# Attention pairs: values behind the next pair's transposes, with copies, shifts and plan steps in other slots

## The chip, the cores and the metric

The kernel runs on one core of a Trainium2 chip. The metric is the device time of one execution in microseconds. The core's engines work side by side, each through its own list of instructions in order: TensorE (PE, matmuls and transposes into PSUM), VectorE (DVE), ScalarE (ACT), GpSimd (POOL) and SyncE (SP, which here issues DMAs). They wait for each other through semaphores.

## What is computed

Causal attention over 8 batches, 12 heads, 448 positions and 64 columns per head, then a mixture of 8 experts with one expert per token and room for 80 tokens each:

```python
scores = scale * np.matmul(q, k.transpose(0, 1, 3, 2))
scores = np.where(mask, -1000000000.0, scores)
attn = np.exp(scores - np.max(scores, axis=-1, keepdims=True))
attn = attn / (np.sum(attn, axis=-1, keepdims=True) + 1e-09)
x = np.matmul(attn, v)            # then (B * S, H * D)
expert_idx = np.argmax(x @ w_gate, axis=1)
# per expert the 80 tokens of largest gate weight:
h = np.maximum(x[tok_idx] @ w1[e], 0.0)
out[tok_idx] = gate_w[tok_idx, None] * (h @ w2[e])
```

## The kernel before, in words

Attention takes the heads two at a time: 8 batches of 6 pairs, 48 pairs in a row, and each pair goes through a software pipeline of three periods. Pair i in its own period: its scores are already in PSUM, and for each of seven blocks of queries DVE runs a *shift* (L445: adds the mask, scales, and takes the extreme of each row) and ACT a *power* (L449: the exponential with the row sum). Blocks 0 and 1 are 192 wide, 2 and 3 are 320, 4 and 5 are 448, the last is 64. In the next period PE *transposes* the powers in four groups of four 128x128 blocks (L483), and each group is *copied* from PSUM to the table PT, the first three whole groups by ACT, the fourth partly by ACT and then partly by DVE (L488). In the period after that PE forms the pair's *values* from PT and v (L506, 16 instructions), and DVE copies them to `xu` (L511, the value copy). Meanwhile PE forms the scores of pair i + 1 (L426) as the last thing in period i, and a small remainder of pair i's scores (L433, `first`) as the first.

A period is written out as eight slots, k = 0 to 7 (the loop at L993 to L1051). All engines' instructions are recorded in the order of this text, and each engine runs its own in that order. Tables say what stands in which slot: TSLOT for the four groups of transposes of pair i - 1, COPIED for their copies, SHIFTED for the seven shifts of pair i; power x always stands in slot x. VSLOT and XSLOT of the new version say it for the values and the value copy; before, values stand in slot 0 and the value copy in slot XSLOT.

Beside the pairs a *plan* runs (`batch_plan`, L943): when a batch's six pairs are through, its steps are put into slots counted from the batch's end, eight per period, so that the steps of one batch share the periods of the next: division by the row sums (NORMS: guard and two small copies on ACT, an inversion on DVE), the transposes of the result into rows and their scaled *stores* (ROWS0 and ROWS1: for each of eight pieces the slot of the turn on PE, L602, and of the store on DVE, L621, whose row then goes out through SP), and the selection of tokens (STEPS; EARLY for the last batch but one): gate products `gp`, their copy `gs`, logits `lp`, `lg`, `logit`, the choice of expert, the ranking with a table of the best 80 so far (`r0t` to `c0l`: two turns on PE, the comparison of the table `rl`/`lt` with lower counts, four comparisons `c3w`/`c3l` to `c0w`/`c0l` of weights on PE and DVE, `gt`), and the merging of new entries (`places` to `row`). Steps that write PSUM and the transposes and the values all take their tiles from one pool `ps_g` of four banks, in turn (L86, L92).

POOL splits q and k into high and low halves for the thirds of a batch to come (L370, L402); DVE does so in the first batch. Behind attention comes a tail for the last batch in a written order (TAIL), then the expert stage, whose weights are loaded through SP into buffers that attention frees.

Of the kernel before, what the change touches and what calls it, by code (L numbers as in the profile page):

```python
# [19 lines left out]
QB = 64  # L20
MASKED = -8.0e9
HUGE = 3.0e38
TSLOT = [1, 2, 4, 5]
COPIED = {2: (0, 0), 3: (1, 0), 4: (2, 0), 5: (3, 0), 6: (3, 1)}
SHIFTED = [0, 0, 1, 1, 2, 3, 3]
XSLOT = 2
NORMS = [0, 2, 2]
ROWS0 = [(2, 4), (4, 5), (6, 7), (10, 12)]
ROWS1 = [(26, 28), (28, 29), (34, 36), (42, 44)]
STEPS = {'gp': 12, 'gs': 13, 'lp': 16, 'lg': 20, 'logit': 20, 'shifted': 21, 'chosen': 22, 'sums': 23, 'one_hot': 23, 'weight': 23, 'columns': 23, 'weighted': 24, 'parts': 24, 'r0t': 29, 'r0c': 30, 'r1t': 30, 'r1c': 31, 'rl': 33, 'lt': 36, 'c3w': 36, 'c3l': 37, 'c2w': 38, 'c2l': 39, 'cp': 41, 'ro': 44, 'c1w': 42, 'c1l': 44, 'c0w': 44, 'c0l': 45, 'gt': 49, 'own': 52, 'earlier': 46, 'rank': 53, 'rr': 55, 'places': 60, 'tn': 66, 'tab': 68, 'rp': 70, 'row': 71}  # L30
EARLY = {'gp': 12, 'gs': 13, 'lp': 16, 'lg': 20, 'logit': 20, 'shifted': 21, 'chosen': 22, 'sums': 23, 'one_hot': 23, 'weight': 23, 'columns': 23, 'weighted': 24, 'parts': 24, 'r0t': 29, 'r0c': 30, 'r1t': 30, 'r1c': 31, 'rl': 33, 'lt': 36, 'c3w': 34, 'c3l': 36, 'c2w': 36, 'c2l': 37, 'c1w': 38, 'c1l': 38, 'cp': 39, 'ro': 40, 'c0w': 39, 'c0l': 40, 'gt': 42, 'own': 44, 'earlier': 41, 'rank': 44, 'places': 45, 'rr': 46, 'tn': 49, 'tab': 49, 'rp': 52, 'row': 53}
THIRD = [0, 0, 2, 2, 4, 6, 8]
THIRD_EARLY = [0, 2, 4, 6, 6, 8, 9]
SECOND = [5, 6, 7, 8, 9, 10, 11]
# [13 lines left out]
def attention_then_moe(  # L48
# [194 lines left out]
    lg = keep.tile([P, NT, H * E], F32, name="lg")  # L243
# [722 lines left out]
    with tc.manual_schedule():  # L966
# [25 lines left out]
        parts = []  # L992
        for i, pr in enumerate(pairs):  # L993
            bt = pr.bt
            if pr.p == 0:
                bt.xu = spool.tile([P, NP, S], F32, name="xu", tag="xu")
                bt.sums = spool.tile([P, NO * H + NP], F32, name="sums", tag="sums", bufs=3)
                bt.rl = None
                for other in pairs[i:i + NP]:
                    other.xu, other.sums = bt.xu, bt.sums  # L1000
                if bt.b < B - 1:
                    batch_plan(bt)
            h = i // PH
            if i % PH == 0:
                if i == 0:
                    later_on(4, [lambda: load_third(2)])
                elif h + 2 < NTH:
                    load_third(h + 2)
                if h:
                    load_values(h)  # L1010
                    if h + 1 < NTH:
                        third_plan(h + 1, i * SLOTS + 1)
            if i == 0:
                scores = scores_groups(pr, i)
                scores[0]()
            _, first, afters = scores
            turns = transpose_groups(pairs[i - 1], i - 1) if i else []
            values = values_group(pairs[i - 2]) if i >= 2 else None
            for k in range(SLOTS):
                if k == 0:  # L1020
                    if values:
                        values[0]()
                    first()
                if turns and k in TSLOT:
                    turns[TSLOT.index(k)][0]()
                for x, at in enumerate(SHIFTED):
                    if at == k:
                        if values and k == XSLOT:
                            values[1]()
                        afters[x][0]()  # L1030
                if k < len(afters):
                    afters[k][1]()
                if turns and k in COPIED:
                    g, x = COPIED[k]
                    turns[g][1][x]()
                for f in plan.pop(i * SLOTS + k, []):
                    f()
                if k == SLOTS - 1 and i + 1 < n:
                    scores = scores_groups(pairs[i + 1], i + 1)
# [386 lines left out]
```

## Time and profile before

| what | us |
|---|---|
| median of 3 runs (508.1 to 512.4) | 508.84 |
| the profiled execution | 507.38 |
| its span, first to last instruction | 505.7 |
| PE busy | 435.1 |
| ACT busy | 399.5 |
| DVE busy | 384.5 |
| POOL busy | 240.8 |
| first power of the first pair, end of the last pair's last power | 8.23, 361.44 |

The span is some 8 us of start, 353 us of attention in 48 periods, and 144 us of tail and expert stage. A busy time is the union of an engine's instructions and says nothing of which wait ends last in a stage; for that one needs a stretch of the timeline, where each row has in brackets how long its engine stood idle before it and what ended that.

### The profile page before, as it was taken

What the parts mean: (1) busy time and instruction counts of PE and PEld (TensorE: products, weight loads), DVE (VectorE), ACT (ScalarE), POOL (GpSimd) and SP (SyncE); (2) the same over time, 40 slices, a digit from 0 to 9 for tenths busy, and PEclk for the clock granted to TensorE, in tenths of its full rate; (3) what the DMA queues carried; (4) which work ended last, traced back from release to release, by engine and by line L of the source; (5) the groups of instructions that cost most, each with busy time, mean ns of one, the idle gap of its engine ahead of it and who ended that gap; (6) DMA issues with size and microseconds to landing.
All of it is one profiled execution on the core that took longest, in us unless ns stands there. A gap on an engine that the chain in (4) does not pass through costs nothing.

```text
span 505.7 us, 15362 instructions
## 1 busy us (share of the span) xinstructions
PE 435.1 (86%) x5530; PEld 330.8 (65%) x5530; DVE 384.5 (76%) x1305; ACT 399.5 (79%) x1081; POOL 240.8 (48%) x345
## 2 busy tenths in 40 slices
PE   2877888898888989888898988888789998999895
PEld 1545656665665666666566666656556998989794
DVE  4655767767877877787787678778668899999991
ACT  4688778878877887887788788778658899989981
POOL 6747426446373745637374563731145135642501
PEclk9999999999999999999999999999999999999999
DMA  6443366564565645545564545536953999999951
GB/s 215 164 170 113 97 214 224 175 204 154 188 200 189 220 149 168 164 172 202 181 218 151 158 158 189 201 110 234 403 230 110 346 391 392 395 389 405 402 209 40
DMA packets 46668, 109.91 MB, mean 217 GB/s; under 512 B 5842, under 2 KB 23250, under 8 KB 45952
## 3 DMA queue, kind: packets, MB, share of 16 engines
q1 hardware_dynamic: 45392, 105.20, 59.1%
q0 software_dynamic: 1056, 3.51, 2.2%
q8 instruction: 43, 0.70, 0.6%
q10 hardware_dynamic: 144, 0.23, 0.2%
q14 instruction: 33, 0.27, 0.2%
HBM read 85.35 MB, written 23.99 MB: 216 GB/s over the span
## 4 chain that ended last, share of the span: by engine, by line
PE 59%; ACT 19%; issue 10%; DVE 8%; DMA 1%; POOLq 0%; ACTq 0%; POOL 0%; DVEq 0%
PE xp L506 18%; ACT prob L449 12%; PE tp L483 8%; ACT PT L488 7%; PE sp L426 5%; DVE ns L445 3%; PE hp L1224 3%; PE gp L556 3%; PE hp L1233 3%; PE hp L1231 3%; PE hp L1234 2%; PE op L1231 2%; PE op L1233 2%; PE op L1234 2%; PE rt L602 2%
## 5 line engine op out<-in xcount | busy, mean ns | idle before, releaser
L449 ACT ACTIVATE prob<-ns,nb 128x192 f32<-128x192 f32 (+3 forms) x336 | 177.8, 530 | 43.5 <-DVE nb L445 42.3
L445 DVE CUSTOM_DVE_ANT_0 ns<-sp,mask 128x192 f32<-128x192 f32 (+3 forms) x336 | 131.8, 440 | 4.4 <-PE sp L433 3.1
L488 ACT COPY PT<-tp 128x512 f32<-128x512 f32 x192 | 101.0, 526 | 28.9 <-PE tp L483 26.0
L506 PE MATMUL xp<-PT,vt 128*64 128x448 f32 (+3 forms) x768 | 93.6, 385 | 30.7 <-ACT prob L449 11.7
L483 PE MATMUL tp<-ident,prob 128*128 128x128 f32 x768 | 111.5, 280 | 9.5 <-ACT PT L488 9.0
L506 PEld LDWEIGHTS xp<-PT,vt 128*64 128x64 f32 x768 | 57.1, 136 | 80.4 <-ACT prob L449 30.4
L370 POOL TENSOR_TENSOR qk<-qk,qk 128x448 f16<-128x448 f32 x93 | 98.5, 1074 | 13.2 <-PE xp L506 8.6
L483 PEld LDWEIGHTS tp<-ident,prob 128*128 128x128 f32 x768 | 84.3, 142 | 25.0 <-ACT PT L488 14.9
L1155 DVE SCALAR_TENSOR_TENSOR wl<-wraw,wh 128x768 f16<-128x768 f32 (+1 forms) x98 | 97.1, 1057 | 2.2 <-POOL wl L1346 1.6
L1170 ACT ACTIVATE wh<-wraw 128x768 f16<-128x768 f32 (+1 forms) x98 | 84.7, 924 | 3.9 <-PE hp L1234 1.3
L488 DVE COPY PT<-tp 64x128 f32<-64x128 f32 x96 | 23.1, 278 | 73.2 <-ACT PT L488 73.2
L426 PE MATMUL sp<-qk 64*128 64x448 f16 (+2 forms) x864 | 70.1, 304 | 7.1 <-DVE qk L381 5.4
L1231 PEld LDWEIGHTS <-wh 128*128 128x128 f16 x668 | 67.1, 100 | 2.6 <-issue 2.5
L1234 PEld LDWEIGHTS <-wl 128*128 128x128 f16 x668 | 66.7, 100 | 2.0 <-issue 1.9
L1233 PEld LDWEIGHTS <-wh 128*128 128x128 f16 x668 | 66.6, 100 | 2.0 <-issue 1.9
L449 ACT ACTIVATION_READ_ACCUMULATOR prob<-ns,nb 128x1 f32 x336 | 63.9, 190 | 0.0
L1312 POOL DMA_INDIRECT out<-yo,idx x8 | 34.2, 4272 | 55.6 <-ACT yo L1309 52.5
L426 PEld LDWEIGHTS <-qk 64*128 64x128 f16 x864 | 36.9, 95 | 29.2 <-issue 10.9
L402 POOL CAST qk<-qk 128x896 f16<-128x896 f32 x40 | 38.8, 988 | 13.3 <-PE sp L433 8.9
L511 DVE COPY xu<-xp 128x448 f32<-128x448 f32 x48 | 29.9, 622 | 19.2 <-PE xp L506 18.8
L1231 PE MATMUL op<-hh,wh 128*128 128x80 f16 x324 | 37.0, 202 | 1.6 <-issue 1.6
L1233 PE MATMUL op<-hl,wh 128*128 128x80 f16 x324 | 37.0, 202 | 1.3 <-issue 1.3
(175 smaller groups left out, 664.0 us busy)
## 6 DMA issues: line engine op xcount, KB each, us to landing
wraw<-w SPq DMA_DIRECT2D x48, 384.0 KB, 9.4
wraw<-w SPq DMA_DIRECT2D x30, 512.0 KB, 9.8
out<-mask SPq DMA_DIRECT2D x56, 192.0 KB, 2.2
qk<-k_t SPq DMA_DIRECT2D x23, 448.0 KB, 3.7
qk<-q_t SPq DMA_DIRECT2D x23, 448.0 KB, 4.8
vt<-v_t SPq DMA_DIRECT2D x24, 384.0 KB, 5.8
xs<-xr SPq DMA_DIRECT2D x42, 192.0 KB, 2.0
wraw<-w SPq DMA_DIRECT2D x5, 1536.0 KB, 9.4
```

What stands on the lines that cost most here:

```text
L370: sub = lambda e, o, a, b: e.tensor_tensor(out=o, in0=a, in1=b, op=ALU.subtract)
L426: nc.tensor.matmul(pr.sp[t, j], a[rows, p, queries(t)], c[rows, p, FROM[t]:FROM[t] + WIDTH[t]], start=(x == 0), stop=(x == 2))
L445: nc.vector.tensor_tensor_reduce(out=ns, in0=pr.sp[x], in1=m, scale=-1.0 / 8.0, scalar=HUGE, op0=ALU.add, op1=ALU.min, accum_out=nb)
L449: nc.scalar.activation(pr.P[:, OFF[x]:OFF[x] + w], got[0], AF.Exp, bias=got[1], scale=-1.0, accum_out=pr.sums[:, h:h + 1])
L483: nc.tensor.transpose(tp[:, i * P:(i + 1) * P], f, ident)
L488: way(part_of(pr.PT, rows, to, *todims), part_of(got[0], rows, at, *dims))
L506: nc.tensor.matmul(xp[rows, c * P:S], st["vt"][:, c, p * P + j * DH:p * P + (j + 1) * DH], pr.PT[:, j, n0:n0 + w], start=(c == 0), stop=(c ...
L1155: return nc.vector.scalar_tensor_tensor(out=l, in0=src, scalar=SW, in1=h, op0=ALU.mult, op1=ALU.subtract)
L1170: nc.scalar.activation(h, src, AF.Copy, scale=SW)
L1231: nc.tensor.matmul(o, wh[:, ws], ah[:, c, :], start=(x == 0 and i % per == 0), stop=False, skip_group_check=True)
L1233: nc.tensor.matmul(o, wh[:, ws], al[:, c, :], start=False, stop=False, skip_group_check=True)
L1234: nc.tensor.matmul(o, wl[:, ws], ah[:, c, :], start=False, stop=(x == n - 1), skip_group_check=True)
```

## The change

Values of pair i - 2 go from slot 0 to slot 5 of the period, behind the four groups of transposes of pair i - 1, which start in slot 0 instead of 1. The value copy goes from slot 2 to slot 6. The first three copies of transposes come one slot sooner, and within a slot the copies now stand ahead of the power instead of behind it. The seven shifts, before all in slots 0 to 3, are spread over slots 0 to 5. Every step of the plan has a new slot; the four steps of the last batch but one that fall behind the loop stay.

```diff
 QB = 64
 MASKED = -8.0e9
 HUGE = 3.0e38
-TSLOT = [1, 2, 4, 5]
-COPIED = {2: (0, 0), 3: (1, 0), 4: (2, 0), 5: (3, 0), 6: (3, 1)}
-SHIFTED = [0, 0, 1, 1, 2, 3, 3]
-XSLOT = 2
-NORMS = [0, 2, 2]
-ROWS0 = [(2, 4), (4, 5), (6, 7), (10, 12)]
-ROWS1 = [(26, 28), (28, 29), (34, 36), (42, 44)]
-STEPS = {'gp': 12, 'gs': 13, 'lp': 16, 'lg': 20, 'logit': 20,
...
+TSLOT = [0, 1, 2, 4]
+COPIED = {1: (0, 0), 2: (1, 0), 3: (2, 0), 5: (3, 0), 6: (3, 1)}
+SHIFTED = [0, 0, 2, 3, 4, 5, 5]
+VSLOT, XSLOT = 5, 6
+NORMS = [0, 1, 2]
+ROWS0 = [(3, 4), (9, 10), (12, 14), (27, 28)]
+ROWS1 = [(35, 36), (40, 41), (43, 44), (44, 46)]
+STEPS = {'gp': 16, 'gs': 18, 'lp': 24, 'lg': 25, 'logit': 26,
...
 THIRD = [0, 0, 2, 2, 4, 6, 8]
 THIRD_EARLY = [0, 2, 4, 6, 6, 8, 9]
 SECOND = [5, 6, 7, 8, 9, 10, 11]
             values = values_group(pairs[i - 2]) if i >= 2 else None
             for k in range(SLOTS):
                 if k == 0:
-                    if values:
-                        values[0]()
                     first()
                 if turns and k in TSLOT:
                     turns[TSLOT.index(k)][0]()
+                if values and k == VSLOT:
+                    values[0]()
                 for x, at in enumerate(SHIFTED):
                     if at == k:
-                        if values and k == XSLOT:
-                            values[1]()
                         afters[x][0]()
-                if k < len(afters):
-                    afters[k][1]()
                 if turns and k in COPIED:
                     g, x = COPIED[k]
                     turns[g][1][x]()
+                if values and k == XSLOT:
+                    values[1]()
+                if k < len(afters):
+                    afters[k][1]()
                 for f in plan.pop(i * SLOTS + k, []):
                     f()
                 if k == SLOTS - 1 and i + 1 < n:
```

PE in the fourth period after a batch's end before, from the end of the scores through values, `first`, two groups of transposes and the first row turn:

```order
L426 MATMUL sp<-qk_0_125 128x448
L506 MATMUL xp<-PT_114,vt_111 64x448 x2
L506 MATMUL xp<-PT_114,vt_111 64x320 x2
L506 MATMUL xp<-PT_114,vt_111 64x192 x2
L506 MATMUL xp<-PT_114,vt_111 64x64 x2
...
L433 MATMUL sp<-qk_0_125,corner_119 128x64
L483 MATMUL tp<-ident,prob_107 128x128 x8
L602 MATMUL rt<-ident,xu 128x128 x3
L483 MATMUL tp<-ident,prob_107 128x128 x4
```

And now in the same period, from the second and third group of transposes over the last row turn to the next pair's scores:

```order
L483 MATMUL tp<-ident,prob_107 128x128 x8
...
L602 MATMUL rt<-ident,xu 128x128 x3
L483 MATMUL tp<-ident,prob_107 128x128 x4
L506 MATMUL xp<-PT_114,vt_111 64x448 x2
L506 MATMUL xp<-PT_114,vt_111 64x320 x2
L506 MATMUL xp<-PT_114,vt_111 64x192 x2
L506 MATMUL xp<-PT_114,vt_111 64x64 x2
L426 LDWEIGHTS qk_1_126
L426 MATMUL sp<-qk_1_126 128x192
```

The values stood between the scores and the transposes; they now stand between the fourth group of transposes and the next pair's scores.

ACT in a calm pair before (prob is written by powers, PT by copies, tp are transposes):

```order
L449 ACTIVATE prob_107,sums<-ns,nb 128x192 x2
L449 ACTIVATE prob_107,sums<-ns,nb 128x320
L488 COPY PT_114<-tp 128x2x256
L449 ACTIVATE prob_107,sums<-ns,nb 128x320
L488 COPY PT_114<-tp 128x2x256
L449 ACTIVATE prob_107,sums<-ns,nb 128x448
L488 COPY PT_114<-tp 128x4x128
L449 ACTIVATE prob_107,sums<-ns,nb 128x448
L488 COPY PT_114<-tp 64x2x2x64
L449 ACTIVATE prob_107,sums<-ns,nb 128x64
```

And now:

```order
L449 ACTIVATE prob_107,sums<-ns,nb 128x192
L488 COPY PT_114<-tp 128x2x256
L449 ACTIVATE prob_107,sums<-ns,nb 128x192
L488 COPY PT_114<-tp 128x2x256
L449 ACTIVATE prob_107,sums<-ns,nb 128x320
L488 COPY PT_114<-tp 128x4x128
L449 ACTIVATE prob_107,sums<-ns,nb 128x320
L449 ACTIVATE prob_107,sums<-ns,nb 128x448
L488 COPY PT_114<-tp 64x2x2x64
L449 ACTIVATE prob_107,sums<-ns,nb 128x448
L449 ACTIVATE prob_107,sums<-ns,nb 128x64
```

The first copy stood behind the third power and stands behind the first now; the fourth group's copy stood ahead of the last power and stands ahead of the last two.

DVE before, at the end of a period, from the last shift to the next pair's first:

```order
L445 ISA ns,nb<-sp,mask_86 128x64
L445 ISA nb 128x1
L621 TENSOR_TENSOR xr<-rt,sums 128x384 x2
L488 COPY PT_113<-tp 64x2x64 x2
L738 COPY ex<-selt 24x512 x2
L445 ISA ns,nb<-sp,mask 128x192
```

And now, from a row store in slot 4 to the next pair's first shift:

```order
L621 TENSOR_TENSOR xr<-rt,sums 128x384
L445 ISA ns,nb<-sp,mask 128x448
L445 ISA nb 128x1
L445 ISA ns,nb<-sp,mask_86 128x64
L445 ISA nb 128x1
L488 COPY PT_114<-tp 64x2x64 x2
L511 COPY xu<-xp 128x448
L445 ISA ns,nb<-sp,mask 128x192
```

The stores and the copies of the selection have left the end of the period, the value copy has come there, and a store stands ahead of the shifts of slot 5.

## Rows read from the trace of the kernel before

**Rows 1.** Busy time in stretches: from the first power of a batch to that of the next, the fourth batch, and the sum over seven such batches (51.45 to 361.44). Columns: the stretch and its length, busy us (and instructions) of PE, PEld, DVE, ACT and POOL, granted clock, DMA share, GB/s.

```profile
139.96:184.23 44.27, 39.60 (x403) 27.67 (x401) 33.91 (x147) 35.94 (x114) 23.51 (x38) 1.00 0.55 180
...
sum 309.99, PE 274.93 PEld 191.98 DVE 234.33 ACT 250.92 POOL 151.68; mean PE 39.28 PEld 27.43 DVE 33.48 ACT 35.85 POOL 21.67
```

**Rows 2.** The same view from each pair's first power to the next one's: a calm pair of the first batch, then six pairs in a row (the first to the sixth period after a batch's end).

```profile
37.16:44.28 7.12, 5.21 (x55) 3.80 (x53) 4.79 (x20) 5.75 (x18) 3.81 (x5) 1.00 0.10 36
139.96:148.62 8.66, 7.72 (x78) 5.37 (x76) 6.04 (x25) 6.46 (x21) 6.38 (x9) 1.00 0.59 209
148.62:154.93 6.31, 6.31 (x66) 3.98 (x62) 5.10 (x20) 6.17 (x20) 3.55 (x4) 1.00 0.41 119
154.93:163.52 8.59, 7.32 (x80) 5.14 (x80) 6.22 (x30) 5.86 (x20) 1.95 (x6) 1.00 0.75 249
163.52:170.43 6.91, 6.36 (x69) 4.82 (x67) 5.21 (x22) 5.75 (x18) 6.55 (x13) 1.00 0.39 116
170.43:177.43 7.00, 6.31 (x66) 4.29 (x63) 6.27 (x31) 5.84 (x19) 3.08 (x5) 1.00 0.81 284
177.43:184.23 6.80, 5.58 (x62) 4.07 (x60) 5.06 (x24) 5.86 (x19) 2.00 (x4) 1.00 0.30 73
```

**Rows 3.** Timeline around that calm pair, in order of time. Columns: start, duration, engine, line, operation, what is written and read, count, and in brackets the engine's idle time before it with what ended it. Powers are L449, shifts L445, copies of transposes L488, the value copy L511, values L506, transposes L483.

```profile
36.90 1.95 PE L506 MATMUL xp<-PT,vt 128*64 128x448 f32 x16 [1.86 <-ACT prob L449]
...
37.16 0.45 ACT L449 ACTIVATE prob<-ns,nb 128x192 f32<-128x192 f32 x1 [0.42 <-DVE nb L445]
...
37.62 0.44 ACT L449 ACTIVATE prob<-ns,nb 128x192 f32<-128x192 f32 x1
...
38.05 0.55 ACT L449 ACTIVATE prob<-ns,nb 128x320 f32<-128x320 f32 x1
...
38.88 1.94 PE L483 MATMUL tp<-ident,prob 128*128 128x128 f32 x16
38.88 0.62 DVE L511 COPY xu<-xp 128x448 f32<-128x448 f32 x1 [0.18 <-PE xp L506]
39.42 0.61 DVE L445 CUSTOM_DVE_ANT_0 ns<-sp,mask 128x448 f32<-128x448 f32 x1
39.60 0.59 ACT L488 COPY PT<-tp 128x512 f32<-128x512 f32 x1 [0.91 <-PE tp L483]
...
40.08 0.56 ACT L449 ACTIVATE prob<-ns,nb 128x320 f32<-128x320 f32 x1
...
40.64 0.57 ACT L488 COPY PT<-tp 128x512 f32<-128x512 f32 x1
...
41.11 0.68 ACT L449 ACTIVATE prob<-ns,nb 128x448 f32<-128x448 f32 x1
...
41.77 0.58 ACT L488 COPY PT<-tp 128x512 f32<-128x512 f32 x1
42.24 0.68 ACT L449 ACTIVATE prob<-ns,nb 128x448 f32<-128x448 f32 x1
...
43.03 0.37 ACT L488 COPY PT<-tp 64x256 f32<-64x256 f32 x1
...
43.43 0.48 DVE L488 COPY PT<-tp 64x128 f32<-64x128 f32 x2 [2.16 <-ACT PT L488]
...
43.84 0.34 DVE L445 CUSTOM_DVE_ANT_0 ns<-sp,mask 128x192 f32<-128x192 f32 x1
...
44.28 0.46 ACT L449 ACTIVATE prob<-ns,nb 128x192 f32<-128x192 f32 x1 [0.41 <-DVE nb L445]
```

**Rows 4.** Timeline of ACT in the second pair of the program.

```profile
16.33 0.46 ACT L449 ACTIVATE prob<-ns,nb 128x192 f32<-128x192 f32 x1 [1.64 <-DVE nb L445]
...
16.78 0.44 ACT L449 ACTIVATE prob<-ns,nb 128x192 f32<-128x192 f32 x1
...
18.26 0.59 ACT L488 COPY PT<-tp 128x512 f32<-128x512 f32 x1 [0.40 <-PE tp L483]
```

**Rows 5.** Groups by line and shape in one steady batch (139.96 to 184.23): busy us, mean ns of one, idle us of the engine just before them and what ended it.

```profile
L483 PE MATMUL tp<-ident,prob 128*128 128x128 f32 x96 | 14.2, 278 | 1.2 <-ACT PT L488 1.2
...
L602 PE MATMUL rt<-ident,xu 128*128 128x128 f32 x24 | 4.0, 275 | 0.2 <-DVE own L823 0.2
...
L621 DVE TENSOR_TENSOR xr<-rt,sums 128x384 f32<-128x384 f32 x6 | 3.2, 551 | 0.0
...
L792 DVE TENSOR_TENSOR rm<-ro,slots_e 80x640 bf16<-80x640 f16 x1 | 1.0, 1022 | 0.0
...
L749 PE MATMUL rn<-ex 128*128 128x512 bf16 x1 | 0.4, 376 | 0.4 <-ACT PT L488 0.4
...
L541 ACT COPY rql<-sums 64x6 f32<-64x6 f32 x2 | 0.4, 196 | 0.3 <-DVE sums L535 0.3
...
L529 ACT ACTIVATE sums<-sums,tiny 128x42 f32<-128x42 f32 x1 | 0.3, 316 | 0.0
...
L765 PE MATMUL rl<-row,ex 128*128 128x80 bf16 x4 | 0.3, 200 | 0.0
```

**Rows 6.** Busy time in a stretch of the expert stage.

```profile
400.00:450.00 50.00, 47.34 (x1006) 46.25 (x1003) 50.00 (x58) 46.08 (x72) 26.85 (x6) 1.00 1.03 386
```

**Rows 7.** Timeline of PE in the last batch.

```profile
350.95 0.66 PE L483 MATMUL tp<-ident,prob 128*128 128x128 f32 x4 [0.61 <-ACT PT L488]
```

More of the change, by code (lines that the diff above doesn't have):

```diff
@@ L22 @@
 HUGE = 3.0e38
-TSLOT = [1, 2, 4, 5]
-COPIED = {2: (0, 0), 3: (1, 0), 4: (2, 0), 5: (3, 0), 6: (3, 1)}
-SHIFTED = [0, 0, 1, 1, 2, 3, 3]
-XSLOT = 2
-NORMS = [0, 2, 2]
-ROWS0 = [(2, 4), (4, 5), (6, 7), (10, 12)]
-ROWS1 = [(26, 28), (28, 29), (34, 36), (42, 44)]
-STEPS = {'gp': 12, 'gs': 13, 'lp': 16, 'lg': 20, 'logit': 20, 'shifted': 21, 'chosen': 22, 'sums': 23, 'one_hot': 23, 'weight': 23, 'columns': 23, 'weighted': 24, 'parts': 24, 'r0t': 29, 'r0c': 30, 'r1t': 30, 'r1c': 31, 'rl': 33, 'lt': 36, 'c3w': 36, 'c3l': 37, 'c2w': 38, 'c2l': 39, 'cp': 41, 'ro': 44, 'c1w': 42, 'c1l': 44, 'c0w': 44, 'c0l': 45, 'gt': 49, 'own': 52, 'earlier': 46, 'rank': 53, 'rr': 55, 'places': 60, 'tn': 66, 'tab': 68, 'rp': 70, 'row': 71}
@@ L31 @@
-EARLY = {'gp': 12, 'gs': 13, 'lp': 16, 'lg': 20, 'logit': 20, 'shifted': 21, 'chosen': 22, 'sums': 23, 'one_hot': 23, 'weight': 23, 'columns': 23, 'weighted': 24, 'parts': 24, 'r0t': 29, 'r0c': 30, 'r1t': 30, 'r1c': 31, 'rl': 33, 'lt': 36, 'c3w': 34, 'c3l': 36, 'c2w': 36, 'c2l': 37, 'c1w': 38, 'c1l': 38, 'cp': 39, 'ro': 40, 'c0w': 39, 'c0l': 40, 'gt': 42, 'own': 44, 'earlier': 41, 'rank': 44, 'places': 45, 'rr': 46, 'tn': 49, 'tab': 49, 'rp': 52, 'row': 53}
+TSLOT = [0, 1, 2, 4]
+COPIED = {1: (0, 0), 2: (1, 0), 3: (2, 0), 5: (3, 0), 6: (3, 1)}
@@ new lines @@
+SHIFTED = [0, 0, 2, 3, 4, 5, 5]
[3 more added lines that the diff above has]
+ROWS1 = [(35, 36), (40, 41), (43, 44), (44, 46)]
+STEPS = {'gp': 16, 'gs': 18, 'lp': 24, 'lg': 25, 'logit': 26, 'shifted': 27, 'chosen': 32, 'sums': 33, 'one_hot': 33, 'columns': 33, 'weight': 35, 'weighted': 36, 'parts': 37, 'r0t': 41, 'r0c': 42, 'r1t': 42, 'r1c': 43, 'rl': 48, 'lt': 50, 'c3w': 50, 'c3l': 51, 'c2w': 56, 'c2l': 57, 'cp': 57, 'c1w': 58, 'ro': 59, 'c1l': 59, 'c0w': 59, 'c0l': 60, 'earlier': 60, 'gt': 65, 'own': 66, 'rank': 66, 'places': 67, 'rr': 69, 'tn': 74, 'tab': 75, 'rp': 80, 'row': 81}
@@ L32 @@
+EARLY = {'gp': 16, 'gs': 18, 'lp': 24, 'lg': 25, 'logit': 26, 'shifted': 26, 'chosen': 28, 'sums': 29, 'one_hot': 29, 'columns': 29, 'weight': 30, 'weighted': 30, 'parts': 30, 'r0t': 32, 'r0c': 33, 'r1t': 33, 'r1c': 34, 'rl': 34, 'lt': 35, 'c3w': 35, 'c3l': 36, 'c2w': 36, 'c2l': 38, 'cp': 40, 'ro': 41, 'c1w': 41, 'c1l': 42, 'c0w': 42, 'c0l': 43, 'earlier': 43, 'gt': 44, 'own': 45, 'rank': 45, 'places': 45, 'rr': 46, 'tn': 49, 'tab': 49, 'rp': 52, 'row': 53}
 THIRD = [0, 0, 2, 2, 4, 6, 8]
```

## The prediction

> **What bounds the kernel now.** I read three views, from coarse to fine. The busy times batch by batch come first: from the second batch on, every batch of six pairs takes the same 44.27 us, with TensorE (PE) busy for 39.60, ScalarE (ACT) for 35.94 and VectorE (DVE) for 33.91 [rows 1]. The reader is to see that no engine is full, and that PE is nearest with 4.67 us of waiting per batch. Then the same batch pair by pair: PE's waiting is not spread evenly, since one pair has none (6.31 busy in 6.31) while others have over a microsecond [rows 2]. Last the timeline of one calm pair, without work of the plan in it, where one can see why a pair with 5.21 us of PE work and 5.75 of ACT work takes 7.12 [rows 2, 3].
>
> The calm pair shows a ring. ACT ends the small copy of the fourth transpose group (43.03 + 0.37), DVE copies the rest of that group (43.43, 0.48), and only then may PE begin the values of that pair, 1.95 us. Behind the values stand the next pair's transposes, and ACT's first copy waits for them by 0.91 us. In the other direction the next shift stands behind DVE's copy, and ACT's first power waits 0.42 us for it. So a period is: values and first transposes with PE alone on the path, then ACT's chain of copies and powers with PE waiting 1.86 us [rows 3].
>
> **The change, part by part.** No instruction's work changes; the sum is one of waits, made against the profiled execution (507.38 us, span 505.7) and then put onto the median, which is 1.46 us above it.
>
> *Values behind the next pair's transposes.* The values at slot 5 read tables that were copied a whole period before, so PE's 1.86 us wait goes. The transposes follow the scores directly, so the 0.91 us of ACT goes too wherever PE is ahead. What is late next: ACT's chain with one link through DVE. From one first power to the small fourth copy, in the new order, with the spacings of rows 3: power 0.46, copy 0.48, power 0.43, copy 0.47, power 0.56, copy 0.47, power 0.56, wide power 0.79, copy 0.37, together 4.59. From there DVE: 0.03 to its copy, 0.41 to the next instruction, 0.54 for the value copy that now stands there (38.88 to 39.42), 0.44 from the shift to the power; together 1.42. Meanwhile ACT's last two powers take some 1.1 of that. The calm pair comes to 6.0 us against 7.12 [rows 2, 3].
>
> There are four calm pairs in the first batch: 4 x 1.12 = 4.5 us gained. In the second pair of the program the new order costs: the first copy now stands ahead of the second and third power, and PE there ended the first transposes late. ACT would wait from 16.78 to 18.26, 1.48 us instead of 0.40 [rows 4]. I take 0.8 of the 1.1 as lost, as a DVE subtraction for the second pair's keys moves into an idle stretch; bounds 0 and 1.1. First batch: 3.7 us gained.
>
> *Copies a half period sooner.* With values last in a period, a period's transposes have only finished powers to wait for: the last power of the pair before ends before the next pair's first begins. The copy stays ahead of a power in ACT's order, so where PE is late ACT idles; where PE is the bound this costs nothing, since ACT's chain from the first copy (4.59 less 0.46, plus two powers) is shorter than a loaded period.
>
> *Shifts over the period, plan steps anew.* The shifts are 0.27 to 0.62 us each and are wanted only by the power of their slot and by the next scores, so spreading them is free as long as DVE isn't held between them. The plan's steps keep clear of slots 6 and 7 but for two stores, so DVE's link above stays short; each store there costs its 0.50 (551 ns less overlap) [rows 5]. On SP the row writes move with their stores. The load of values that is issued at the start of a third waits for values of the pair before last of that buffer, now at slot 5 instead of slot 0; they are over when it is issued, and its data are wanted two pairs later, so nothing queued behind it is held.
>
> *The steady batch.* If PE never waited a batch would take its 39.60 us; that is the lower bound. Two of the six periods after a batch's end are then set by ACT's chain instead. In the first one, ACT has the guard (0.32 less an overlap of 0.1) and two small copies (0.40) on top of 6.0, so 6.6, where PE has 5.21 plus a row turn 0.5, 0.3 and 0.4, so 6.4; in the fifth PE has 5.8 and the chain 6.0 [rows 2, 5]. That adds 0.2 + 0.2: 40.0. For waits on PSUM banks (four in the pool that transposes, values and the plan share) I keep today's 1.2 us per batch, the idle time that the transposes' row puts down to ACT's copies [rows 5]. The bounds are 0, because the copies are sooner, and twice as much, 2.4, because the plan now puts up to 11 tiles into one period (second one) where before the most was 9. So 41.2, with 39.6 and 42.4 as ends. Seven batches: 7 x (44.27 - 41.2) = 21.5 us.
>
> *The rest.* The stage behind attention keeps its length: there DVE is busy for 50.00 of 50 us and the DMA share is 1.03 [rows 6], and its early loads go into buffers that attention frees, so they move with its end. In the last period DVE's copies for the last pair but one stand, as before, behind the placing step of 1.02 us [rows 5], which ACT's later copy covered; that copy comes sooner now, so the step may show, while ACT's chain also ends sooner. I take 0, bounds -1 and +1.
>
> Sum: 3.7 + 21.5 = 25.2 us. 507.38 - 25.2 = 482.2 on the profiled execution's scale, 483.6 on that of the median.
>
> **The rivals.**
>
> *The banks take it back.* For: in the second and sixth period after a batch's end 11 and 10 tiles go through four banks, and in the last batch PE already stood 0.61 us at a transpose for a copy [rows 7]. If each tile beyond seven costs that (4 + 3 + 1 + 1 in four periods), a batch is 40.0 + 5.5 = 45.5; at 0.48 each it is 44.3, and what is left is the first batch, 505. I put this rival at 506. Against: copies now lead, and in the steady batch the same wait is only 1.2 us in all.
>
> *Slower: DVE held at plan steps between shifts.* Eight row stores, four comparisons and the lower-count step now stand among the spread shifts, six of the stores one slot behind their own transposes where before it was three. Every wait there holds the next shift, thus ACT's power and the next scores. It decides from (44.27 - 40.0) / 13 = 0.33 us per step. At the 0.50 that one row turn takes on PE [rows 5], a batch is 40.0 + 6.5 = 46.5 and the time 508.84 + 7 x 2.23 - 3.7 = 520.7. Against: PE's turn comes ahead of the same slot's work, and PE runs ahead of DVE when it is the bound.
>
> *PE is no bound at all.* Weight loads fill only 27.67 of a batch's 44.27 us [rows 1]; if PE's matmuls are merely stretched by waiting and close up when fed, ACT is the bound with 35.94 plus its link, six times 0.25: 37.4, and the time 508.84 - 7 x 6.87 - 3.7 = 457. Against: the pair in which PE had no idle time at all was still 6.31 us long [rows 2]. The Trainium skill (Perfetto Trace Analysis, "Identifying the Most-Contended Engine") speaks for this rival: it calls matmul busy time a bad measure of how near TensorE is to its limit and wants the share of weight loads instead; by that rule PE has a third in hand. Here the rows with PE full say that it doesn't.
>
> **How the numbers follow.** The ring falls and PE, or nearly, becomes the bound: 0.76, with 39.6 to 42.4 per batch, so 508.84 - 32.7 - 4.5 = 472 to 508.84 - 13.1 - 3.4 = 492. Banks: 0.11, spread over 497 to 512. DVE: 0.08. PE no bound: 0.05. One per cent is 5.1 us, about what a measurement of this kernel can tell. Faster by more: 0.76 + 0.04 of the banks' cases + 0.05 = 0.85; within: 0.06; slower: 0.09. A range of 473 to 503 leaves out the last rival, 0.02 of the forecast's lower end, 0.05 of the banks and the slower case: 0.20.
>
> **What would show it.** Right: the calm pairs of the first batch near 6.0 us between first powers, values that start with no wait behind the fourth transposes, and batches near 41 us with PE idle for under 2. The idle time of DVE's copy behind ACT's should stay, as it's off the path. Wrong: PE waits at transposes for copies, of 0.5 us or more at the second and sixth period after a batch's end (banks); idle time of DVE at row stores or comparisons, followed by ACT's powers waiting for their shifts (DVE); PE busy well under 39 us per batch (PE no bound).

## The result, and the profile after

The changed kernel takes 492.45 us (median of 4 runs, 491.35 to 494.14) beside 508.47 for the kernel before on the same chip (4 runs, 507.77 to 512.4): ratio 0.968, 95% interval 0.963 to 0.973. That is 16.0 us gained where 25.2 were forecast, and 8.9 us above the predicted 483.6. The profiled execution is 491.92 us with a span of 490.2, so 15.5 us of span are to be accounted for (505.7 before).

The batches, from the first power of one to that of the next (columns as in [rows 1]): the second, third, fifth, seventh and eighth.

```profile
46.81:86.33 39.52, 36.80 (x357) 24.31 (x356) 29.57 (x127) 35.75 (x114) 21.00 (x32) 1.00 0.54 174
86.33:127.67 41.34, 39.37 (x387) 26.27 (x386) 32.78 (x137) 35.73 (x113) 21.98 (x37) 1.00 0.64 210
...
170.69:213.72 43.03, 40.35 (x403) 27.05 (x402) 35.33 (x147) 35.97 (x114) 23.31 (x38) 1.00 0.56 185
...
256.74:301.40 44.66, 41.98 (x403) 27.67 (x402) 35.40 (x147) 35.95 (x113) 23.29 (x38) 0.96 0.54 178
301.40:344.89 43.49, 40.24 (x403) 26.88 (x401) 37.23 (x161) 36.05 (x113) 14.77 (x29) 1.00 0.62 213
```

Before, the seven batches took 309.99 us together, 44.28 each [rows 1]. Now they take 298.1 (46.81 to 344.89): 11.9 gained, 21.5 forecast. The second batch is under the forecast 41.2 and the third at it; they hold fewer steps of the plan, as the counts of instructions show. The fourth to the sixth, where the plan is complete, take 43.02 each; "full batch" means such a one from here on. The seventh is the same batch with 1.64 us more PE time at a granted clock of 0.96, and is taken up at the end. The first batch gained 4.64 (its end came from 51.45 to 46.81), the stage behind attention took 145.3 instead of 144.3. 4.64 + 11.91 - 1.05 = 15.5.

Pair by pair, first the calm pair that answers to 37.16 of before, then the six of the fifth batch (answers to [rows 2]):

```profile
34.59:40.70 6.11, 5.47 (x55) 3.60 (x54) 4.99 (x20) 5.74 (x18) 4.45 (x6) 1.00 0.25 79
170.69:177.43 6.74, 5.94 (x59) 3.91 (x57) 5.98 (x30) 6.35 (x21) 3.53 (x5) 1.00 0.85 268
177.43:185.01 7.58, 7.25 (x73) 5.04 (x72) 6.22 (x27) 5.86 (x18) 2.15 (x4) 1.00 0.32 114
185.01:193.95 8.94, 8.94 (x91) 5.59 (x90) 6.52 (x22) 6.39 (x19) 5.22 (x7) 1.00 0.81 264
193.95:200.31 6.36, 5.13 (x57) 3.17 (x55) 5.77 (x24) 5.74 (x18) 0.77 (x2) 1.00 0.23 58
200.31:206.62 6.31, 6.31 (x68) 4.72 (x67) 4.91 (x26) 5.87 (x19) 4.88 (x10) 1.00 0.85 304
206.62:213.72 7.10, 6.79 (x68) 4.61 (x66) 5.93 (x23) 5.75 (x19) 6.76 (x12) 1.00 0.24 87
```

The calm pair went from 7.12 to 6.11, as the forecast 6.0 had it. Of the loaded pairs, those where PE is busy all the time (185.01 and 200.31) stand beside others with 0.3 to 1.2 us of waiting: 2.68 per batch, against the 4.67 of before and the 1.6 of the forecast. The longest of them, the third, is 8.94.

The calm pair in order of time (columns as in [rows 3]):

```profile
34.59 0.46 ACT L449 ACTIVATE prob<-ns,nb 128x192 f32<-128x192 f32 x1 [0.29 <-DVE nb L445]
...
35.16 0.59 ACT L488 COPY PT<-tp 128x512 f32<-128x512 f32 x1
...
35.80 1.95 PE L506 MATMUL xp<-PT,vt 128*64 128x448 f32 x16 [0.58 <-ACT PT L488]
...
38.92 0.37 ACT L488 COPY PT<-tp 64x256 f32<-64x256 f32 x1
...
39.32 0.48 DVE L488 COPY PT<-tp 64x128 f32<-64x128 f32 x2 [1.12 <-ACT PT L488]
39.73 0.61 DVE L511 COPY xu<-xp 128x448 f32<-128x448 f32 x1
...
40.26 0.34 DVE L445 CUSTOM_DVE_ANT_0 ns<-sp,mask 128x192 f32<-128x192 f32 x1
...
40.70 0.46 ACT L449 ACTIVATE prob<-ns,nb 128x192 f32<-128x192 f32 x1 [0.29 <-DVE nb L445]
```

The ring is gone: ACT's copy at 35.16 follows its power without a wait (0.91 before). Values start at 35.80; their wait of 0.58 ends with ACT's first copy, which frees a PSUM bank, and no longer with the copies of their own pair. In [rows 3] the wait of 1.86 stands with ACT's last power as its end, since that and DVE's copy end within 0.05 us of each other; the next pair's row names DVE's copy:

```profile
44.06 1.24 PE L506 MATMUL xp<-PT,vt 128*64 128x448 f32 x6 [1.91 <-DVE PT L488]
```

The forecast had the values start with no wait behind the fourth transposes; in the calm pair that wasn't so. What is late now is the link forecast: small copy on ACT (38.92), DVE's copy (39.32), value copy (39.73), shift (40.26), power (40.70). From the first power to DVE's copy 4.73 us (forecast 4.62), from there to the next power 1.38 (forecast 1.42).

ACT in the second pair of the program (answers to [rows 4]):

```profile
15.34 0.46 ACT L449 ACTIVATE prob<-ns,nb 128x192 f32<-128x192 f32 x1 [1.34 <-DVE nb L445]
...
17.24 0.59 ACT L488 COPY PT<-tp 128x512 f32<-128x512 f32 x1 [1.35 <-PE tp L483]
```

ACT does wait 1.35 us for the first transposes there, as forecast (1.48), but the pair starts 0.99 us sooner than before, at 15.34 instead of 16.33.

Groups by shape in the fifth batch (answers to [rows 5]):

```profile
L483 PE MATMUL tp<-ident,prob 128*128 128x128 f32 x97 | 14.4, 278 | 0.6 <-DVE ro L783 0.3 <-ACT PT L488 0.2
```

Transposes wait 0.6 us instead of 1.2. The third pair, the one of 8.94, shows two other things: the placing step L792, 1.02 us before, takes 1.70, and DVE stands 2.38 us at `own`, the step that takes the rank of a token's weight from PE's product `gt`:

```profile
185.43 1.70 PE L556 MATMUL gp<-xu,wgd 128*32 128x448 f32 x12
...
187.56 0.40 PE L802 MATMUL gt<-oh,less 128*128 128x8 bf16 x10
...
187.99 0.19 DVE L823 TENSOR_TENSOR own<-gt,goh 128x32 f32<-128x32 f32 x1 [2.38 <-PE gt L802]
...
188.32 0.48 DVE L445 CUSTOM_DVE_ANT_0 ns<-sp,mask 128x320 f32<-128x320 f32 x1
...
188.70 3.62 POOL L370 TENSOR_TENSOR qk<-qk,qk 128x448 f16<-128x448 f32 x3
...
188.72 1.70 DVE L792 TENSOR_TENSOR rm<-ro,slots_e 80x640 bf16<-80x640 f16 x1
...
190.34 0.61 DVE L445 CUSTOM_DVE_ANT_0 ns<-sp,mask 128x448 f32<-128x448 f32 x1
...
190.70 1.72 PE L426 MATMUL sp<-qk 64*128 64x192 f16 x18
...
191.06 0.67 ACT L449 ACTIVATE prob<-ns,nb 128x448 f32<-128x448 f32 x1 [0.71 <-DVE nb L445]
...
191.57 1.09 DVE L841 TENSOR_TENSOR rr<-rank,slots_t 128x320 bf16<-128x320 f16 x1
```

PE has the gate products (185.43, 1.70 us, slot 16 of one batch's plan) ahead of `gt` (187.56, slot 65 of the plan of the batch before: the same period, one slot later). DVE has `own` in its list ahead of four shifts. So it stands 2.38 us, the shift at 188.32 and those from 190.34 on come late, ACT's power waits 0.71 for them and the next scores, which need the buffers that shifts free, take 1.72 (1.40 in e1_gt_first below). ACT's waits for shifts in the whole batch (in total, times, longest):

```profile
ACT prob L449 <- DVE nb L445: 6.4, 9, 1.3
```

That is the theory for the missing 1.8 us per full batch: **DVE is held at `own`, between spread shifts**. The rival: nothing holds at one place; PE's waits at PSUM banks, which the forecast had at 1.2 us, are simply larger.

### The profile page after: what moved, and what is told of

Its sections match the earlier page's. It is cut to its first block, busy times and chain, and to the rows that moved or that the text cites. A ratio compares the mean times of both kernels' runs of the same rounds, so it can differ in the third digit from the quotient of the medians.

```text
span 490.2 us, 15235 instructions
## 1 busy us (share of the span) xinstructions
PE 441.8 (90%) x5530; PEld 325.1 (66%) x5530; DVE 392.7 (80%) x1305; ACT 400.5 (82%) x1081; POOL 235.3 (48%) x345
## 4 chain that ended last, share of the span: by engine, by line
PE 52%; DVE 19%; ACT 14%; issue 8%; DMA 3%; POOL 2%; SPq 0%; POOLq 0%; ACTq 0%; DVEq 0%
PE xp L506 12%; ACT prob L449 7%; DVE ns L445 6%; ACT PT L488 6%; PE sp L426 6%; PE tp L483 5%; PE hp L1224 3%; DMA vt<-v_t 3%; PE gp L556 3%; PE hp L1231 3%; PE hp L1233 3%; PE hp L1234 3%; PE op L1231 3%; PE op L1233 2%; PE op L1234 2%
## 5 line engine op out<-in xcount | busy, mean ns | idle before, releaser
L449 ACT ACTIVATE prob<-ns,nb 128x192 f32<-128x192 f32 (+3 forms) x336 | 177.9, 531 | 42.7 <-DVE nb L445 41.2
L445 DVE CUSTOM_DVE_ANT_0 ns<-sp,mask 128x192 f32<-128x192 f32 (+3 forms) x336 | 138.0, 441 | 3.8 <-PE sp L426 1.6
L483 PE MATMUL tp<-ident,prob 128*128 128x128 f32 x768 | 112.5, 279 | 6.7 <-ACT PT L488 3.8
L488 ACT COPY PT<-tp 128x512 f32<-128x512 f32 x192 | 101.2, 528 | 15.2 <-PE tp L483 12.4
L506 PE MATMUL xp<-PT,vt 128*64 128x448 f32 (+3 forms) x768 | 95.3, 391 | 6.9 <-ACT PT L488 4.7
L483 PEld LDWEIGHTS tp<-ident,prob 128*128 128x128 f32 x768 | 83.8, 141 | 20.3 <-ACT PT L488 7.6
L506 PEld LDWEIGHTS xp<-PT,vt 128*64 128x64 f32 x768 | 51.6, 138 | 53.3 <-issue 24.7
L426 PE MATMUL sp<-qk 64*128 64x448 f16 (+2 forms) x864 | 71.6, 304 | 6.9 <-DVE qk L381 5.4
L449 ACT ACTIVATION_READ_ACCUMULATOR prob<-ns,nb 128x1 f32 x336 | 64.2, 191 | 0.0
L1312 POOL DMA_INDIRECT out<-yo,idx x8 | 29.8, 3720 | 60.4 <-ACT yo L1309 51.5
L488 DVE COPY PT<-tp 64x128 f32<-64x128 f32 x96 | 23.0, 277 | 33.1 <-ACT PT L488 32.4
L1231 PE MATMUL hp<-xh,wh 128*128 128x80 f16 x320 | 36.3, 202 | 1.9 <-issue 1.8
L402 POOL CAST qk<-qk 128x896 f16<-128x896 f32 x40 | 36.2, 934 | 3.0 <-PE sp L426 3.0
```

The source lines that it names most:

```text
L426: nc.tensor.matmul(pr.sp[t, j], a[rows, p, queries(t)], c[rows, p, FROM[t]:FROM[t] + WIDTH[t]], start=(x == 0), stop=(x == 2))
L445: nc.vector.tensor_tensor_reduce(out=ns, in0=pr.sp[x], in1=m, scale=-1.0 / 8.0, scalar=HUGE, op0=ALU.add, op1=ALU.min, accum_out=nb)
L449: nc.scalar.activation(pr.P[:, OFF[x]:OFF[x] + w], got[0], AF.Exp, bias=got[1], scale=-1.0, accum_out=pr.sums[:, h:h + 1])
L483: nc.tensor.transpose(tp[:, i * P:(i + 1) * P], f, ident)
L488: way(part_of(pr.PT, rows, to, *todims), part_of(got[0], rows, at, *dims))
L506: nc.tensor.matmul(xp[rows, c * P:S], st["vt"][:, c, p * P + j * DH:p * P + (j + 1) * DH], pr.PT[:, j, n0:n0 + w], start=(c == 0), stop=(c ...
```

## Experiments

Twelve kernels ran; ratios are against runs of the kernel before on the same chip. The full batch is the fifth, the calm pair the mean of the last four of the first batch.

| run | edit | us | ratio, 95% | full batch | calm pair |
|---|---|---|---|---|---|
| the change | | 492.45 | 0.963 to 0.973 | 43.03 | 6.11 |
| e1_gt_first | `gt` a slot sooner | 485.80 | 0.954 to 0.960 | 42.11 | 6.11 |
| e2_rank_dve | `rank` on DVE | 488.31 | 0.959 to 0.965 | 42.56 | 6.11 |
| e3_invert_later | inversion a slot later | 491.84 | 0.964 to 0.972 | 43.09 | 6.11 |
| e4_all_three | those three | 486.28 | 0.954 to 0.960 | 42.17 | 6.11 |
| e6_shifts_front | shifts as before | 486.79 | 0.959 to 0.964 | 42.14 | 6.10 |
| e9_gt_and_shifts | e1 and e6 | 487.30 | 0.958 to 0.965 | 42.38 | 6.11 |
| e7_old_plan | plan as before | 490.44 | 0.966 to 0.970 | 42.77 | 6.11 |
| e10_old_plan_gates_later | the same, gate steps later | 489.87 | 0.963 to 0.968 | 42.72 | 6.11 |
| e11_old_plan_shifts_front | the same, shifts as before | 489.61 | 0.962 to 0.967 | 42.49 | 6.11 |
| e5_values_front | values in slot 0 | 543.59 | 1.071 to 1.075 | 50.91 | 6.42 |
| e8_values_alone | before, values moved alone | 528.37 | 1.040 to 1.045 | 47.00 | 6.76 |
| e12_values_alone_gates_later | the same, gate steps later | 519.26 | 1.020 to 1.026 | 46.36 | 6.76 |

**What holds the full batch.** One slot for `gt`, an addition of 128x4 numbers taken from POOL, one slot for the inversion of the sums, and all of them:

```diff
# e1_gt_first
-'earlier': 60, 'gt': 65, 'own': 66
+'earlier': 60, 'gt': 64, 'own': 66
# e2_rank_dve
-eng.tensor_tensor(out=bt.rank, in0=bt.rank, in1=bt.larger, op=ALU.add)
+nc.vector.tensor_tensor(out=bt.rank, in0=bt.rank, in1=bt.larger, op=ALU.add)
# e3_invert_later
-NORMS = [0, 1, 2]
+NORMS = [0, 2, 2]
# e4_all_three: the three edits together
```

> One plan step of the changed kernel moves one slot ahead: the counting products on PE (gt) from slot 65 to 64, so that they stand ahead of the gate products of 1.7 us instead of behind them. Theory A (DVE is held: its step own waits 2.4 us for gt and the shifts of slots 3 to 5 stand behind it): the wait falls under 0.8 us, the powers and with them the next period's products come sooner, a full batch goes from 43.0 to 42.0 us, and over five full batches the kernel gains some 5 us, 487.5. Rival B (in that period PE is full for 7.59 us, so DVE's wait is cover and costs nothing): the wait falls, the batch stays at 43.0 and the time at 492.5.

> The step rank of the changed kernel runs on DVE instead of POOL, so that POOL no longer waits 4.4 us for it and releases three subtractions of q and k all at once. Theory C (POOL and DVE block each other at two-input operations on SBUF: the placing step took 1.70 instead of 1.02 us and the rank comparison 1.09 instead of 0.47): both go back to 1.02 and 0.47, the products that wait for the comparison come sooner by up to 0.86, a full batch goes from 43.0 to 42.2 and the time to 488.5. Rival D (the longer durations have another cause, such as their place in the period): they stay at 1.7 and 1.1, and the time at 492.5.

> The inversion of the row sums stands in slot 2 again instead of slot 1, behind a shift, so that DVE no longer waits 0.62 us for ACT's guard in the first period after a batch's end. Theory A (held DVE): the lower-count step comes sooner and PE's wait of 0.70 us for its PSUM bank at the row turn shrinks to some 0.2; a full batch goes from 43.0 to 42.6, the time to 490. Rival (banks: PE waits there whatever DVE does, since eight tiles share four banks): the 0.70 stays and so does the time.

> All three edits together: counting products ahead of the gate products, rank on DVE, inversion in slot 2. Theories A and C: a full batch near 41.2 us, the time 482 to 485. Rival B: 43.0 and 492, or what one of the edits gives alone.

DVE in e1_gt_first, the same pair:

```profile
185.60 0.19 DVE L823 TENSOR_TENSOR own<-gt,goh 128x32 f32<-128x32 f32 x1 [0.16 <-PE gt L802]
...
186.34 1.70 DVE L792 TENSOR_TENSOR rm<-ro,slots_e 80x640 bf16<-80x640 f16 x1
...
189.19 1.09 DVE L841 TENSOR_TENSOR rr<-rank,slots_t 128x320 bf16<-128x320 f16 x1
191.49 0.48 DVE L488 COPY PT<-tp 64x128 f32<-64x128 f32 x2 [1.20 <-ACT PT L488]
```

and its fifth batch (columns as in [rows 1]):

```profile
170.52:212.63 42.11, 39.95 (x403) 27.17 (x402) 35.42 (x147) 35.84 (x113) 23.32 (x38) 1.00 0.57 189
```

`own` waits 0.16 instead of 2.38, DVE is now early (at 191.49 it waits for ACT again), and the batch is 0.92 shorter, as expected. All of it is in the third pair, which takes 8.03 instead of 8.94; ACT's waits for shifts come to 4.1 us in the batch instead of 6.4. With 0.35 more PE time than before and 2.16 of PE waiting it is still 0.9 above the forecast 41.2.

In the change POOL had stood at `rank` for `own`'s result and then ran three subtractions from 188.70 to 192.32, beside DVE's L792 and L841. In e2_rank_dve they no longer meet:

```profile
L370 POOL TENSOR_TENSOR qk<-qk,qk 128x448 f16<-128x448 f32 x13 | 13.3, 1040 | 0.2
...
L792 DVE TENSOR_TENSOR rm<-ro,slots_e 80x640 bf16<-80x640 f16 x1 | 0.8, 810 | 0.0
...
L841 DVE TENSOR_TENSOR rr<-rank,slots_t 128x320 bf16<-128x320 f16 x1 | 0.5, 480 | 0.0
```

L792 falls from 1.70 to 0.81 and L841 from 1.09 to 0.48, while `own` still waits 2.38, and the batch gains 0.47, about half of what was expected. In e1_gt_first both steps still take 1.70 and 1.09, but DVE has the time: e4_all_three, where they take 0.81 and 0.57, is no shorter. It was expected at 41.2 and gave 42.17, so the two cures are for the same hold. e3_invert_later took away the wait it was made for (a row turn's 0.70 us for DVE is gone from PE's rows), and PE then stood 0.67 us at the values of the same period, for ACT's copies. So a bank that comes free sooner there only shows the next one.

**Which part carries the gain.** From the change: values back in slot 0; shifts back; the plan of before. From before: values moved alone.

```diff
# e5_values_front: the change, but
-VSLOT, XSLOT = 5, 6
+VSLOT, XSLOT = 0, 2
# e6_shifts_front: the change, but
-SHIFTED = [0, 0, 2, 3, 4, 5, 5]
+SHIFTED = [0, 0, 1, 1, 2, 3, 3]
# e7_old_plan: the change, but NORMS, ROWS0, ROWS1, STEPS, EARLY of before with
-'gp': 12, 'gs': 13
+'gp': 14, 'gs': 15
# e8_values_alone: before, with the same two numbers and the value steps moved to
+VSLOT, XSLOT = 5, 6
```

> The change with the values back in slot 0, which is now behind the first group of transposes (the text puts a slot's transposes ahead of its values), and the value copy in slot 2; copies, shifts and plan steps stay as changed. If the ring (small copy, DVE's copy, values, next copy) is what the change took away: the values wait again for DVE's copy of the pair before, with one group of transposes ahead of them, so a calm pair of the first batch goes from 6.1 to about 6.5 us and the full batch from 43.0 to about 44; the time about 499. If the earlier copies and the spread shifts carry the gain by themselves: calm pairs 6.1, full batch 43.0, time 492.

> The change with the seven shifts back in slots 0 to 3; everything else as changed. If the spread shifts are held by plan steps (the theory of the held DVE): shifts stand ahead of the waiting step `own` and of row stores, full batch 43.0 to about 42.2, time about 487. If the spread costs nothing and its place between copies is needed by the value copy: full batch 43.0 or more, calm pairs unchanged or longer, time 492 or more.

> The change with the plan's slots of before (the two gate steps at 14 and 15, so that they come behind the values of their batch, which are later now). Values, copies and shifts stay as changed. If the new plan carries part of the gain: calm pairs stay 6.1, full batch from 43.0 to between 44 and 45.5, time about 500 to 508. If the plan's place is of no matter: 43.0 and 492; if the old plan is better, because gate products don't stand ahead of `gt` in it: 42 and 486.

> The kernel before with its values moved to slot 5 behind the transposes and the value copy to slot 6 (the two gate steps at 14 and 15, behind the values of their batch); transposes, copies, shifts and the other plan steps as before. If the values' place is the main part of the gain: calm pairs from 7.12 to about 6.5 (the small copy still stands ahead of the last power only, so DVE's copy comes later than in the change), full batch from 44.27 to about 43.5, time about 500. If the copies' earlier slots are needed for it: calm pairs about 7.0, full batch about 44.3, time about 507.

e6_shifts_front gained what e1_gt_first did: `own` still waits 1.43, but only two shifts stand behind it instead of four, and the batch is 42.14. e7_old_plan is no worse than the change, 42.77: the new plan doesn't carry the gain.

The surprise is on the other side. Values moved alone make the kernel 4% slower, and the change with its values in slot 0, between the first and the second group of transposes, is 7% slower, though the calm pair is shorter than before in both. Neither expectation had a kernel slower than before. Part of e8_values_alone is its gate copy, on which ACT stood 1.61 us per batch, so that was moved in a second set of runs:

```diff
# e9_gt_and_shifts: the change, with the edits of e1_gt_first and e6_shifts_front
# e10_old_plan_gates_later: e7_old_plan, but
-'gp': 14, 'gs': 15, 'lp': 16
+'gp': 16, 'gs': 18, 'lp': 19
# e11_old_plan_shifts_front: the same and SHIFTED = [0, 0, 1, 1, 2, 3, 3]
# e12_values_alone_gates_later: e8_values_alone with these gate steps
```

> The change with the `gt` step one slot sooner and the seven shifts back in slots 0 to 3, both at once; everything else as changed. If both remedies free the same thing (shifts held behind `own`), they don't add: full batch 42.1, time about 486. If there are two holds, one at `own` and one at row stores: full batch 43.0 - 0.9 - 0.9 = 41.2, time about 480.

> The change with the plan of before, and the gate steps at slots 16, 18 and 19, where their copy doesn't stand ahead of a power that is due. In the run with the gate steps at 14 and 15 ACT stood 0.95 us in each batch at that copy. If that wait was on the path: full batch 42.8 to about 41.8, time about 484, so the respread plan was a loss. If it wasn't: 42.8, 490.

> The same with the shifts back in slots 0 to 3, so that of the change only the places of values and copies and the order of copy and power are left. If spreading the shifts costs by itself (every plan step between them can hold them): about 0.9 less per full batch than the run with the spread shifts beside it, near 41.0, time about 479. If it costs only where `own` is late, as in the new plan: no difference to that run, about 41.8 and 484.

> The kernel before with the values and the value copy moved alone, and the gate steps at slots 16, 18 and 19. If the loss of the first run of this kind (528 us) came from the gate copy, on which ACT stood 1.61 us per batch: full batch 47.0 - 1.6 = 45.4 at best, time about 515, still over that of before, because row turns then wait for the late copies of transposes (1.4 to 2.1 us each time). If the values' place alone is a gain once the gate steps are out of the way: full batch under 44.3, time under 506.

e9_gt_and_shifts shows again that the cures don't add (42.38). In e10_old_plan_gates_later the 0.95 of ACT at the gate copy went, and the batch stayed at 42.72: the gate products only moved their time into the next period (the second and third pair take 6.11 and 9.02 instead of 7.99 and 7.22). e11_old_plan_shifts_front, with the spread shifts undone, is 0.23 per batch shorter than e10, where in the new plan the same edit gave 0.89. So spreading shifts costs where a step of the plan is late between them, as the second theory of that run had it, and little elsewhere.

e12_values_alone_gates_later is 9 us better than e8_values_alone, with 0.64 per batch of the 1.61, and still 12 us worse than before. Its calm pair, from the end of one period to the next one's first power:

```profile
47.69 0.37 ACT L488 COPY PT<-tp 64x256 f32<-64x256 f32 x1
...
48.09 0.48 DVE L488 COPY PT<-tp 64x128 f32<-64x128 f32 x2 [3.14 <-ACT PT L488]
...
48.50 0.61 DVE L511 COPY xu<-xp 128x448 f32<-128x448 f32 x1
...
49.47 0.46 ACT L449 ACTIVATE prob<-ns,nb 128x192 f32<-128x192 f32 x1 [0.94 <-DVE nb L445]
```

The link is the one of the change, but the small copy stands behind the wide powers, so nothing covers it: from 48.09 to 49.47 ACT does one small power and waits 0.94. ACT's waits for shifts in a loaded batch (in total, times, longest):

```profile
ACT prob L449 <- DVE nb L445: 10.8, 7, 1.8
```

That is 10.8 us at seven powers, where the change has 6.4 at nine. DVE's waits for PE in e5_values_front, in the batch from 191.57:

```profile
DVE lg L582 <- PE lp L570: 3.5, 1, 3.5
...
DVE xr L621 <- PE rt L602: 2.7, 1, 2.7
DVE less L752 <- PE rn L749: 2.5, 1, 2.5
DVE row L872 <- PE rp L868: 2.2, 1, 2.2
```

With values in front, the products that PE makes for the plan come behind their 1.95 us, and the steps of DVE that take these products stand between the spread shifts: `lg`, row store, `less` and `row` wait 10.9 us together. That is DVE held between shifts, as in the slower rival of the prediction, though `lg` and `row` aren't among the thirteen steps that it counted. What follows from it is not the sign that it named: ACT's powers wait only 2.8 us for their shifts. PE's scores wait for shifts instead, and ACT's copies, which now lead the powers, for transposes that stand behind the values:

```profile
ACT PT L488 <- PE tp L483: 9.8, 6, 2.6
...
PE sp L426 <- DVE nb L445: 5.6, 9, 1.3
```

The batch is beyond the rival's price too, 50.91 for 46.5. Some 1.2 of it is a granted clock of 0.97 (an estimate: the fourth pair takes 9.58 there and 8.39 in the eighth batch, where the clock stays at 1.00). How the rest divides between the two waits wasn't tried, nor were values in front with the earlier copies and the plan and shifts of before.

## Why the prediction was right, and where it was too good

*Values behind the transposes, copies sooner: right.* Calm pairs 6.11 for 6.0, with both links as worked out. The prediction took the copies' earlier slots as free extras; the runs show that they are the condition. With the plan and the shifts of before (e12 and e11, both with the gate steps later), the values' place alone gives 46.4 per full batch, and with the earlier transposes and copies 42.5 (before: 44.27). The change without its values' place is at 50.9, with the new plan and spread shifts in it. So new plan and spread shifts together cost 0.5 per full batch (42.49 to 43.03). What each half does alone couldn't be read off the ring, since the other half covers its link.

*The first batch: 4.64 for 3.7, in part by chance.* The four calm pairs gained 4.1 us for the 4.5 forecast, and the second pair took 0.44 longer (7.05 for 6.61) for the 0.8: together 3.65. The other 0.99 is the first pair, which the prediction left out. There POOL waits for a DMA at the start, which lands at another time in every run (POOL goes on between 11.45 and 12.21): in the timeline of POOL, the copy of the corner that waits for it (L375) starts at 11.50 in the change, at 12.21 before, and at 12.14 in e1_gt_first, whose first pair is that of the change. From that copy to the second pair's first power it takes 3.84 us in the change, 3.83 in e1_gt_first, and 4.12 before and in e6_shifts_front, whose shifts are those of before. So 0.28 of the 0.99 comes with the spread shifts, and 0.71 is luck of the profiled execution.

*The steady batch: the term that was mis-sized, 43.03 for 41.2, outside its bounds of 39.6 to 42.4.* Of the 1.83 us, 0.92 is the hold at `own`: the step of the prediction that failed is that spreading the shifts is free "as long as DVE isn't held between them". The gate products' 1.70 us had been moved ahead of `gt` in one period, by numbers that stand far apart in the table (16 of one batch, 65 of the batch before), and this wasn't looked for. It is the mechanism of the slower rival, at a step that is none of the thirteen that the rival counted. The other 0.91 is what e1_gt_first still has: 0.35 more PE time (39.95, forecast 39.60) and 2.16 of PE waiting for 1.6. The term of 1.2 for PSUM banks is too small: it was read from the transposes' row alone. Before, PE waited 0.9 us per batch in the same way at L749 and L602, 2.1 in all; in e1_gt_first such waits still come to 2.0 (0.70 for DVE's lower-count step, 0.33 for its step `ro`, 0.94 for ACT's copies). That they are waits for banks is read from the releasers named. e3_invert_later shows one that gave way only to the next. None of the nine variants of plan and shifts came under 42.1; what sets that floor wasn't settled.

*The account.* First batch 0.9 better; second batch 1.7 better and third 0.1 worse than 41.2; the fourth to sixth 1.8 worse each; the seventh and eighth 3.5 and 2.3 worse; the stage behind attention 1.05 worse: together 9.8 us, where 25.2 - 15.5 is 9.7 (before, the seven batches were 0.1 longer than seven times 44.27). Of the seventh's 3.5, 1.64 is the clock. The second batch was better because it holds less of the plan, whose steps now reach further into the batches behind, and not by the mechanism forecast. The 1.05 wasn't followed up; among e1_gt_first to e4_all_three that stage takes 145.1 to 146.2 us. So the median lies at the upper end of the main forecast (472 to 492) and well inside the range (473 to 503), with a full batch beyond its own bounds. That is luck in part: the first two batches gave 2.6 us that the sum didn't have, and the range holds over half of the banks' cases.

*The rivals.* Banks: PE's waits for them are 2.0 to 2.5 us, not 5.5, and the sign (0.5 us or more at transposes in the second and sixth period) didn't come: 0.33 and 0.23. DVE held: true at `own` for 0.9 us per batch. PE no bound: a batch's PE time stayed at 39.95 to 40.35 when its waits had shrunk to between 2.16 and 2.68 us. Weight loads fill 27.05 of the fifth batch's 43.03 us. By the rule of the Trainium skill (Perfetto Trace Analysis, "Identifying the Most-Contended Engine") a third would be in hand; the trace doesn't agree here, as the matmuls didn't close up when fed.

The shortest version is e1_gt_first, 485.80 us, 0.957 of before (0.954 to 0.960), where the forecast was 0.950 (483.6 of 508.84); e4_all_three is not to be told from it.

## What to carry to other kernels

When instructions are moved behind others in an in-order list, write out for the fullest period what then stands behind each waiting step, with steps of all batches that share it: one table number cost 0.9 us per batch here. And a move that closes one ring opens the next link: price it with and without the companion moves, since the parts of a change can each be a loss (values alone +2.1 us per batch, all but the values' place +6.6) where the whole is a gain (-1.2).

## What the runs showed of the hardware

*DVE and POOL hold each other up.* The subtractions of POOL and DVE's L792 and L841 take longer when they meet: in the change L792 takes 1.70 us against 0.81 in e2_rank_dve, L841 1.09 against 0.48, and three of POOL's subtractions in a row 3.62 against 3.03. Which of the two is held differs: in e6_shifts_front L841 takes 0.48 beside three subtractions that take 4.01. The Trainium skill (SBUF — State Buffer, "SBUF: two separate sides") says that a DVE operation with two inputs in SBUF and a GpSimd operation that reads SBUF exclude each other for the whole of an instruction. The sizes in the change agree: L792 and L841 are 0.89 and 0.61 longer, and one subtraction takes 1.04. It cost time only where DVE was late already (0.47 per batch in the change, nothing in e1_gt_first).

*The granted clock falls for some microseconds in the middle of steady work.* In e8_values_alone the fourth batch (its fourth pair; 171 to 177 us) and the fifth at the same place (221 us):

```profile
171.00:173.00 2.00, 1.52 (x9) 0.97 (x11) 1.03 (x2) 2.00 (x7) 2.00 (x4) 0.89 0.29 104
173.00:175.00 2.00, 2.00 (x8) 0.71 (x6) 0.48 (x2) 1.53 (x6) 2.00 (x4) 0.50 0.96 272
175.00:177.00 2.00, 2.00 (x26) 1.48 (x24) 0.78 (x2) 0.00 (x0) 1.94 (x3) 0.76 0.96 364
...
221.00:223.00 2.00, 2.00 (x19) 1.08 (x17) 0.21 (x2) 1.95 (x7) 2.00 (x3) 1.00 1.04 315
```

PE had waited 1.36 and 0.48 us just before (at 169.6 to 172), as it did in the fifth batch, where the clock stayed at 1.00. In the fourth it went to 0.50, its level of 1.2 GHz, and the 16 values took 3.60 us instead of 1.95; the batch is 48.64 against 47.00. Four of that run's 48 pairs and one of the changed kernel's (the fourth pair of the seventh batch, 1.65 us) show it. Why the same pattern brings it in one batch and not in the next stays open.
